# The first q transposed by DMA, the filter in six transfers, and a searched order at the start of a one-core attention and gating kernel

## Chip, cores and metric

One core of one Trainium2 chip. The metric is device microseconds (us) of one execution; lower is better. A run is told "slow" where it is more than 1.5% above the fastest run of the same kernel in the same comparison. The executions of this kernel scatter by 2 to 3% within one session, without a gap between fast and slow, so each comparison carries its own runs of the kernel before, on the same chip, and a 95% interval.

## The reference, cut

```python
def phi(x):                                   # q, k: [8 batches, 8 heads, 576, 64]; w_phi: [64, 128]
    proj = np.einsum('bhsd,df->bhsf', x, w_phi)
    proj = proj - np.max(np.abs(proj), axis=-1, keepdims=True)
    return np.concatenate([np.exp(proj), np.exp(-proj)], axis=-1)
q_p, k_p = (phi(q), phi(k))
kv = np.einsum('bhsf,bhsd->bhfd', k_p, v)     # one key-value product per head
z = np.sum(k_p, axis=2)
x = (q_p @ kv) / (q_p . z + 1e-6)             # shortened; then heads side by side: [8, 576, 512]
x1, x2, x3 = np.split(x @ w_proj, 3, axis=-1)
conv = irfft(rfft(x2, axis=1) * rfft(filter_fft, axis=0))   # filter_fft: [576, 512]
out = (x1 * conv * x3) @ w_out
```

## The kernel before

Every operation is a short method, and one long string of words, PLAN, gives the order in which they are issued; an engine, an index or a PSUM bank ("@4") stands in the word. Each engine takes its own instructions in that order. The parts that matter here:

```python
PLAN = """
zeros w_load,phi w_phi loadh,k,0,0 gen_rows gen_cols,1 loadh,k,0,1 gen_ident warm,10,4@0 T,k,0,0,1@0
gen_cols,0 Te,DVE,k,0,0,1@0 T,k,0,0,0@2 Te,ACT,k,0,0,0@2 filt_load,SP,1 warm,2,4@1 warm,3,1@1
T,k,0,1,0@4 loadh,q,0,0 Pk,0,0@0 Pk,0,1@2 ex,k,m,0,1@2 Te,ACT,k,0,1,0@4 gen_selidx loadh,q,0,1
load,k,1 gen_pads ... T,q,0,0,1@4 warm,5,4@5 T,q,0,1,1@5
Te,DVE,q,0,1,1@5 gen_turns,POOL,0 exkt,p,0@6 T,q,0,0,0@6 Te,DVE,q,0,0,1@4 T,q,0,1,0@4 ex,k,p,0,1@2
Te,ACT,q,0,0,0@6 warm,4,4@2 Qn,0,0@6 Te,ACT,q,0,1,0@4 load,v,0 ...
... load,q,1 ... vs,POOL,p,0,0 maxk,0,2@4 filt_load,SP,0 gen_sin,1 load,v,1 ...
vs,POOL,m,0,0 warm,18,4@6 warm,2,1@6 KV,0,0@4 KVe,DVE,0,0@4 trm,0 Pq,0,0@0 trh,q,1,1 ...
"""   # some 1,900 words more

def load(self, n, b):            # q, k or v of one batch from DRAM: 512 rows of 1152 B in bf16, on GpSimd's queue
    self.nc.gpsimd.dma_start(out=..., in_=...)          # loadh: half of the heads

def trh(self, n, b, X):          # a half of q or k, loaded before, transposed within SBUF, on SP's queue
    self.nc.sync.dma_start_transpose(out=self.at(n + "T", b)[:, 9 * X:9 * X + 9, :],
        in_=self.at(n + "n", b)[:, 2 * X:2 * X + 2].rearrange("p v j d -> p (v j d)"))

def T(self, n, b, X, i):         # the same on TensorE, for batch 0: matmuls with the identity
    ...
        self.mm(self.pb(k // 4 % 2, o, o + 128), x[:, c:c + 128], self.at("ident"), True, True)

def Te(self, eng, n, b, X, i):   # and the copy out of PSUM, by ACT or DVE
    ...

def filt_load(self, eng, i):     # one half of the filter, 9 transfers of 32 rows of 2048 B
    q = dict(SP=self.nc.sync, ...)[eng]
    rows = self.dram["filt"][288 * i:288 * i + 288, :].rearrange("(t j) d -> j t d", j=9)
    for k, j in enumerate((0, 2, 4, 6, 1, 3, 5, 7)):
        p = 32 * (k % 4)
        q.dma_start(out=self.fl[i][p:p + 32, k // 4, :], in_=rows[j])
    q.dma_start(out=self.fl[i][0:32, 2, :], in_=rows[8])
```

Qn is q's projection as the maxima need it, maxq the maxima of it, mhi/mlo and trm (mT) turn the maxima into an operand, Pq is the projection that the exponentials (ex) read, vs scales v on GpSimd, KV is the key-value product, warm is filler: matmuls on a tile "idle" that only keep the clock up.

## Time and profile before

| | kernel before |
|---|---|
| median of 3 runs, first session | 327.4 us (324.55 to 330.71) |
| span of the profiled execution | 320.2 us |
| TensorE (PE) busy / of it filler | 293.6 / 18.3 us |
| not useful PE time before 60 us / 60 to 300 / after 300 us | 30.4 / 7.3 / 7.2 us |
| filter transfers: number, KB, issue to landing | 18, 64.0 KB, 5.2 us |

"Not useful" is idle time plus filler. The lines for these are in the prediction below, read there. One view that it does not show: the queue of SP, the engine that issues all transposes and the filter's transfers. In the timeline of SP's queue (start, us that the issue itself took, line, operation, what, how many) the kernel before has:

```profile
2.00 3.85 SPq L420 DMA_DIRECT2D fl<-in_moe_filter_fft_dram  x8
6.81 6.12 SPq L420 DMA_DIRECT2D fl<-in_moe_filter_fft_dram  x8
...
26.47 1.19 SPq L679 DMA_TRANSPOSE mT<-mh  x1
27.76 2.72 SPq L545 DMA_TRANSPOSE qT<-qn  x2
30.57 3.56 SPq L545 DMA_TRANSPOSE kT<-kn  x2
```

The filter is off SP's hands at 13.4 us, and these transposes take 1.2 to 1.8 us each to issue.

### The profile page before, as it was taken

Reading aid. Unit: us, or ns where it says so; the run is one execution under the profiler, and the core shown is the slowest. Engines: PE = TensorE matmul, PEld = TensorE weight load, DVE = VectorE, ACT = ScalarE, POOL = GpSimd, SP = SyncE. Lnnn points to the kernel's source line nnn. Section 1 sums busy time; section 2 is a strip of 40 time slices with the busy share of each in tenths; the row PEclk is TensorE's granted clock in tenths of the full one; section 3 lists DMA queues with packets and bytes.
Section 4 is the critical chain, followed back from the end, with each engine's and each line's share of the span. In section 5 each row is a group of like instructions: output and inputs, shape, how many; then the busy total and the mean of one; then the engine's idle time right before and its main releaser. Section 6 shows DMA issues by size and latency. Waiting matters only on the chain.

```text
span 320.2 us, 9561 instructions
## 1 busy us (share of the span) xinstructions
PE 293.6 (92%) x3971; PEld 162.5 (51%) x3971; DVE 252.6 (79%) x416; ACT 229.4 (72%) x361; POOL 216.8 (68%) x175
## 2 busy tenths in 40 slices
PE   6659779999999899999799999999999999999982
PEld 2434643475465464475355554655566444764430
DVE  3584797699989997999478997888889988667860
ACT  2496999699788887897487875876788756843531
POOL 8769764967585962799084976938988589824140
PEclk9986987999999999999799999999999999999999
DMA  6999999969996999696943499787434410442506
GB/s 115 236 166 167 173 176 167 202 113 174 153 178 100 188 155 219 107 142 99 201 91 89 108 160 164 118 133 150 111 47 90 117 39 0 93 102 50 133 4 159
DMA packets 78667, 41.52 MB, mean 130 GB/s; under 512 B 58976, under 2 KB 73440, under 8 KB 78624
## 3 DMA queue, kind: packets, MB, share of 16 engines
q1 hardware_dynamic: 63808, 24.66, 40.1%
q0 software_dynamic: 14816, 16.25, 33.6%
q8 instruction: 31, 0.51, 0.7%
q14 instruction: 12, 0.10, 0.1%
HBM read 33.75 MB, written 9.44 MB: 135 GB/s over the span
## 4 chain that ended last, share of the span: by engine, by line
PE 74%; DVE 11%; ACT 5%; DMA 5%; issue 2%; POOL 0%; SPq 0%; ACTq 0%; DVEq 0%; POOLq 0%
PE ps L840 16%; PE ps L456 14%; PE ps L797 8%; PE ps L930 7%; PE ps L705 4%; PE ps L726 4%; DVE mq L650 4%; PE ps L296 3%; PE ps L847 2%; PE ps L611 2%; DMA kn<-in_k_dram 2%; DVE mk L650 2%; DMA mT<-mh 2%; PE ps L590 2%; PE ps L617 2%
## 5 line engine op out<-in xcount | busy, mean ns | idle before, releaser
L840 PE MATMUL ps<-xT,wproj 128*128 128x512 bf16 x256 | 64.3, 384 | 0.0
L907 POOL TENSOR_TENSOR yT<-cv,x1s 128x576 bf16<-128x576 f32 x22 | 27.9, 1276 | 36.1 <-DVE cv L897 20.3
L650 DVE TENSOR_REDUCE mq<-ps 128x8 f32<-128x1024 f32 (+1 forms) x40 | 44.0, 1111 | 5.8 <-PE ps L590 2.9
L650 DVE TENSOR_REDUCE mk<-ps 128x8 f32<-128x1024 f32 (+1 forms) x40 | 44.0, 1112 | 5.5 <-PE ps L583 4.5
L690 POOL TENSOR_TENSOR vp<-vn,vp 128x1152 bf16<-128x1152 bf16 x16 | 34.3, 2148 | 13.8 <-DVE yT L907 8.3
L827 POOL TENSOR_TENSOR t<-C,B 128x1024 bf16<-128x1024 bf16 x15 | 31.9, 2126 | 12.9 <-ACT C L710 6.2
L634 ACT ACTIVATE Eqp<-ps 128x1024 bf16<-128x1024 f32 x32 | 32.8, 1030 | 7.9 <-PE ps L617 7.7
L930 PE MATMUL ps<-wout,yT 128*128 128x512 bf16 x144 | 36.7, 380 | 1.4 <-DVE yT L907 0.9
L634 ACT ACTIVATE Ekm<-ps 128x1024 bf16<-128x1024 f32 x32 | 33.0, 1033 | 5.5 <-PE ps L583 4.6
L634 ACT ACTIVATE Eqm<-ps 128x1024 bf16<-128x1024 f32 x32 | 32.7, 1030 | 5.0 <-PE ps L617 4.3
L690 POOL TENSOR_TENSOR vm<-vn,vm 128x1152 bf16<-128x1152 bf16 x16 | 34.3, 2146 | 2.3 <-ACT es L892 1.5
L897 DVE TENSOR_TENSOR cv<-es,ps 128x288 f32<-128x288 f32 x64 | 25.8, 449 | 12.4 <-ACT es L892 10.9
L840 PEld LDWEIGHTS <-wproj 128*128 128x128 bf16 x256 | 22.8, 98 | 24.8 <-issue 1.4
L634 ACT ACTIVATE Ekp<-ps 128x1024 bf16<-128x1024 f32 x32 | 32.6, 1030 | 1.8 <-PE ps L583 1.1
L834 POOL TENSOR_TENSOR Y<-Y,t 128x1024 bf16<-128x1024 bf16 x14 | 29.7, 2123 | 1.9 <-DVE Y L822 1.3
L797 PE MATMUL ps<-wproj,eo 128*128 128x512 bf16 x128 | 29.9, 379 | 0.4 <-DVE eo L781 0.4
L456 PE MATMUL ps<-inv,Y 128*128 128x288 bf16 (+1 forms) x192 | 27.4, 291 | 0.2 <-DVE xnt L757 0.2
L710 ACT COPY o<-ps 128x512 f32<-128x512 f32 x27 | 15.7, 586 | 16.4 <-PE ps L930 11.8
L822 DVE TENSOR_TENSOR Y<-ps,A 128x1024 bf16<-128x1024 f32 (+1 forms) x24 | 24.8, 1041 | 3.0 <-PE ps L456 1.6
L877 DVE TENSOR_TENSOR x1s<-ps,x1s 128x512 bf16<-128x512 f32 x32 | 21.9, 686 | 5.1 <-PE ps L840 4.7
L745 DVE TENSOR_TENSOR xn<-ps,r 128x512 bf16<-128x512 f32 x32 | 22.0, 691 | 1.1
L710 ACT CAST x2n<-ps 128x512 bf16<-128x512 f32 (+1 forms) x28 | 14.5, 524 | 10.9 <-PE ps L797 8.8
(156 smaller groups left out, 632.4 us busy)
## 6 DMA issues: line engine op xcount, KB each, us to landing
out_dram<-o SPq DMA_DIRECT2D x72, 128.0 KB, 2.4
vn<-in_v_dram POOLq DMA_DIRECT2D x8, 576.0 KB, 6.4
kn<-in_k_dram POOLq DMA_DIRECT2D x7, 576.0 KB, 8.6
qn<-in_q_dram POOLq DMA_DIRECT2D x7, 576.0 KB, 7.0
wproj<-in_moe_w_proj_dram POOLq DMA_DIRECT2D x3, 512.0 KB, 7.1
fl<-in_moe_filter_fft_dram SPq DMA_DIRECT2D x18, 64.0 KB, 5.2
kn<-in_k_dram POOLq DMA_DIRECT2D x2, 288.0 KB, 5.7
qn<-in_q_dram POOLq DMA_DIRECT2D x2, 288.0 KB, 8.2
```

The source lines that it names most:

```text
L456: self.mm(self.pb(e, 0, n), l, r, start=(x == same[0]), stop=(x == same[-1]))
L634: self.nc.scalar.activation(e, self.db(), AF.Exp, bias=0.0, scale=1.0 if g == "p" else -1.0)
L650: self.nc.vector.tensor_reduce(out=out, in_=src, axis=AX.X, op=ALU.max, apply_absolute_value=True)
L690: self.port(eng, self.elem(eng).tensor_tensor(out=t[:, :, :, 0:64], in0=self.at("vn", b)[:, 2 * X:2 * X + 2], in1=t[:, :, :, 64:65].to_bro ...
L710: self.nc.scalar.copy(dst, src)
L797: self.mm(self.pb(0), eo[:, kt, 128 * c:128 * c + 128], w[:, kt, 512:1024], start=(kt == 0), stop=(kt == 3))
L827: self.port(eng, self.elem(eng).tensor_tensor(out=self.at("t2", b)[:, t, :], in0=self.at("C", b)[:, o, :], in1=self.at("B")[:, t, :], op=A ...
L834: self.port(eng, self.elem(eng).tensor_tensor(out=Y, in0=Y, in1=self.at("t2", b)[:, t, :], op=ALU.add))
L840: self.mm(self.pb(0), w[:, kt, f0 + 128 * m:f0 + 128 * m + 128], x[:, kt, :], start=(kt == 0), stop=(kt == 3))
L897: self.nc.vector.tensor_tensor(out=self.at("cv", 4 * b + m)[:, :, odd, :], in0=e, in1=o, op=ALU.subtract if odd else ALU.add)
L907: self.port(eng, self.elem(eng).tensor_tensor(out=self.at("yT", b)[:, m, 0:SEQ], in0=self.at("cv", 4 * b + m).rearrange("p j h t -> p (j h ...
L930: self.mm(self.pb(0), y[:, kt, 128 * j:128 * j + 128], w[:, kt, :], start=first and kt == ks[0], stop=last and kt == ks[-1])
```

## The change

Its intent is to shorten the start: take q's transposes and their copies off TensorE and ScalarE, spend less of SP on issuing, make the sine tables early, and load batch 1 before the first scaling of v. The core of the diff:

```diff
 def filt_load(self, eng, i):
-        for k, j in enumerate((0, 2, 4, 6, 1, 3, 5, 7)):
-            p = 32 * (k % 4)
-            q.dma_start(out=self.fl[i][p:p + 32, k // 4, :], in_=rows[j])
+        for odd in range(2):
+            q.dma_start(out=self.fl[i][:, odd, :], in_=rows[odd:8:2])
         q.dma_start(out=self.fl[i][0:32, 2, :], in_=rows[8])
 def T(self, n, b, X, i):            # k of batch 0 only, now
-            self.mm(self.pb(k // 4 % 2, o, o + 128), x[:, c:c + 128], self.at("ident"), True, True)
+            self.nc.tensor.transpose(self.turned(8)[:, o:o + 128], x[:, c:c + 128],
+                                     self.at("ident"))        # bf16, eight in one PSUM bank
 (B: four blocks become two; m3 subtracts for one of them)
 PLAN, first part
-...T,q,0,0,1@4 ... T,q,0,1,1@5 Te,DVE,q,0,1,1@5 ... T,q,0,0,0@6 ... (q of batch 0 on TensorE)
+zeros loadh,k,0,0 w_load,phi gen_rows gen_cols,0 gen_turns,ACT,0 loadh,q,0,0 loadh,k,0,1 gen_ident
+...
+Pkt,0@2 maxkt,0@2 load,v,0 load,q,1 gen_selidx ...
+em,p,0,0 vs,POOL,p,0,0 load,k,2 filt_load,SP,1 ...
+w_load,proj,1 trh,q,0,0 Qn,0,0@2 maxq,0,0@2 filt_load,SP,0 ...
+ex,k,m,0,2@6 trh,q,0,1 Qnt,0@2 ... mhi,0 trh,k,1,1 trh,k,1,0 ...
 (all of PLAN is in another order; filler falls from 53 wide and 17 narrow to 22 and 10)
```

On SP's queue the order is now: half of the filter, first half of q of batch 0, the other half of the filter, second half of q, both halves of k of batch 1, then q of batch 1 and the maxima.

## The prediction

> **What bounds the kernel now.** I read the page's totals first, then busy time by stage, the chain that ended last, and the timeline and the DMA view of the start. The totals say that TensorE is the engine to watch:
>
> ```profile
> PE 293.6 (92%) x3971; PEld 162.5 (51%) x3971; DVE 252.6 (79%) x416; ACT 229.4 (72%) x361; POOL 216.8 (68%) x175
> ...
> PEclk9986987999999999999799999999999999999999
> ```
>
> But 92% is an average over stages. The busy times by stage (length, PE, PEld, DVE, ACT, POOL, granted clock, DMA share, GB/s), first of everything and then of the tile "idle" alone, the operand of the filler matmuls that only keep the clock up:
>
> ```profile
> 0.00:6.00 6.00, 4.53 (x16) 1.67 (x17) 2.13 (x20) 1.28 (x1) 4.74 (x15) 1.00 0.53 93
> 6.00:30.60 24.60, 17.01 (x152) 8.96 (x149) 15.61 (x23) 17.91 (x26) 19.51 (x26) 0.86 1.04 187
> 30.60:47.00 16.40, 12.07 (x340) 9.60 (x338) 13.11 (x25) 14.46 (x18) 11.91 (x11) 0.97 1.20 177
> 47.00:60.00 13.00, 13.00 (x87) 5.18 (x87) 10.01 (x19) 9.62 (x21) 7.62 (x7) 0.78 1.25 180
> 60.00:90.00 30.00, 28.53 (x502) 17.25 (x501) 27.33 (x41) 26.38 (x40) 21.55 (x15) 1.00 1.04 155
> 90.00:300.00 210.00, 205.47 (x2815) 113.92 (x2809) 175.59 (x277) 154.35 (x247) 147.72 (x102) 0.99 0.64 117
> 300.00:320.20 20.20, 12.98 (x83) 5.90 (x81) 8.81 (x17) 5.41 (x11) 3.79 (x3) 0.97 0.40 94
> ```
> ```profile
> 6.00:30.60 24.60, 11.59 (x46) 4.78 (x46) 0.00 (x0) 0.86 1.04 187
> ...
> sum 320.20, PE 18.31 PEld 7.21 DVE 0.11; mean PE 2.62 PEld 1.03 DVE 0.02
> ```
>
> Useful TensorE work is 293.6 - 18.3 = 275.3 us, so 44.9 us of the span are not useful. In the first 60 us PE is busy 46.6 us, of which 17.0 us is filler: 30.4 us lost. From 60 to 300 us it is 6.0 idle plus 1.3 filler, 7.3 us. After 300 us it is 7.2 us. From 60 us on the kernel is simply TensorE bound and a shuffled order has little to win there. Two thirds of the loss is the start, and this change aims at the start.
>
> What holds the start? The chain in order of time (start, us, what):
>
> ```profile
> 2.88 6.93 DMA kn<-in_k_dram
> 9.85 0.62 PE ps L562 x8
> ...
> 16.29 1.83 ACT qT L710 x2
> ...
> 20.78 3.49 DVE mq L650 x3
> 24.31 6.39 PE ps L296 x20
> 30.70 1.26 PE ps L705 x72
> ```
>
> First the second half of k (landed at 9.85), then q's transposes and their copies, then VectorE's maxima; the filler (L296) up to 30.7 us only stands in PE's queue before the first key-value product. From 6 to 30.6 us DVE is idle 9.0, ACT 6.7 and POOL 5.1 of 24.6 us: batch 1 is not there yet. Its q is issued at 19.2 us and its transposes only at 27.8 us.
>
> **What the Trainium skill says.** (1) PSUM — Partial Sum Buffer, Specifications, engine access: a matmul writes fp32 "except transposes, which write the input dtype uncast"; that is what permits eight bf16 transposes in one bank. No transpose of the kernel before does this, so its trace does not show it. (2) TensorE: Matmul & The Clock Gate, Part 1: the clock falls to half after about 3.4 us without enough activity and recovers after about as long. The trace agrees: the granted clock was 0.86 over 6-30.6 us, and 0.78 over 47-60 us behind the thin work of 30-47 us. There 13.0 x 0.22 = 2.9 us of full-speed work was lost. (3) DMA: Bandwidth & Descriptors, "Why a DMA increments its semaphore by 16 and not by 1": a transfer uses the largest number of engines up to 16 that divides the slowest dimension of both sides. The old filter transfers have 32 rows on each side, so 16 engines. The new ones read 4 x 32 rows into 128 partitions, so by this rule 4 engines. No transfer of the kernel before has such a shape; its trace cannot say. (4) Advanced Engine Details and Errata, X-Bar Transpose (TRN2): transposes by DMA are as fast as ordinary ones. The trace agrees: 288 GB/s while a half of q or k is transposed (28-34 us), 230 GB/s for loads (14-19.5 us).
>
> **The change, part by part.**
> - q of batch 0 by DMA: removes 18 PE transposes (1.5 us busy), two 1024-wide ACT copies (1.9 us) and two small DVE ones (0.5 us), and adds two DMA transposes: 0.295 MB each at 288 GB/s is 1.0 us of the DMA engines, 1.3 us of the SP queue, and 3.1 us from issue to landing. It takes 1.8 us of ACT out of the chain but puts about 3 us after q's landing. The first q half is now loaded second, before k's second half, so this wait lies beside k's work. On the path: about -1 to -2 us.
> - bf16 transposes of k: same 18 matmuls, half the banks. The copies read the same 1024 elements; I expect the 1.01 us of ACT and 1.22 us of a DVE cast unchanged. Worth about 0; it frees a bank.
> - Filter in 6 transfers instead of 18: SP's queue spends 0.3-0.8 us on each, so about 6 us less of SP issue, and SP has q0's transposes to issue then. Bytes are the same, 1.18 MB.
> - B halved, subtraction instead of addition: two evictions of 0.59-0.69 us and half of a memset, once, about 1.3 us of ACT/DVE. The 2.13 us POOL multiplies and adds keep their size.
> - Filler: 53 wide and 17 narrow become 22 and 10. At 0.216 us per wide one that is about 7 us of PE, nearly all inside waits. Worth about 0, with a risk of a colder clock.
> - Order: the sine tables and both sine activations move before the first exponential, to where ACT waits for k; before, they take ACT from 22.0 to 27.8 us (two table loads of 1.28, activations of 0.68, 0.61, 0.24, 0.92) in the busiest part. That is worth 3-4 us there. Loads of v0, q1 and k2 are issued before POOL's first scaling, so batch 1 is projected ahead of the first key-value product.
>
> The sum of the start, by counting both orders with the durations above (reduce 1.18, exponential 1.0, scaling of v 2.14, product L705 1.2, 128-wide projection group 0.3, 512-wide group of four 0.86 us). Ahead of batch 2's first key-value product the kernel before has PE 48.1, DVE 69.0, ACT 72.1, POOL 67.6 us, and it is reached at 88.95 us. The changed one has PE 43.0, DVE 70.8, ACT 66.3, POOL 71.2 there; where its PE sum is 48.1, DVE is about 77, ACT 71, POOL 75. So 8 us more of DVE and 7 us more of POOL stand before the same TensorE work. In 0-90 us the kernel before has 68.2 us of DVE busy, so 22 us idle; the new order must cut these to about 10. With the first data at 5.7 us and about 6 us of table arithmetic done while waiting, DVE has some 71 us left from about 10 us on: 81 us with no gaps, 88 us at the 91% which it reached from 60 to 90 us. Between 1 and 8 us earlier; I take 4. Off that: the last matmuls have a little less to stand beside the last halves (two output groups instead of a projection pair and one), 1 us. Total -3 to -4 us of 327.
>
> **Rivals.**
> - A: the start is bound by DMA, and the new order shifts no bytes. From 6 to 60 us the DMA engines show a share of 1.04 to 1.25, i.e. never free. mT of batch 0 now stands on SP's queue behind the first transpose of q1, which waits for q1's load. Ten half loads at 1.28 us, 4.7 us of filter, 4 us of transposes after a start at 3.4 us give q1 at 25 us, as before (19.2 + 5.9). With the filter on 4 engines these would carry 2 x 64 packets more, about 67 ns each (estimate from packet times), 8.6 us instead of 2.4 us: q1 at 30 us, mT at 34 us, and the first query projection at 34 instead of 31.8 us. Then the time is 326-330 us. Against it: DMA has gaps after 25 us.
> - B: the start is bound by ACT and DVE arithmetic, and the order fills it. Then 316-320 us. For it: ACT 9.1 of 10 us busy from 20 to 30 us. Against it: DVE needs over 91%.
> - C: POOL becomes the bound. Eight scalings of v, 17 us, now precede the first filter matmul instead of five, and folds of batches 0 and 1 moved from DVE (0.65 us) to POOL (2.13 us). That would make about 325 us.
> - D: less filler, colder clock: a second stretch at 0.6-0.8 for 10 us costs up to 3 us; 326 us.
>
> **Range and chances.** The reference is 327.4 us, with runs 324.55 to 330.71, a scatter of 2% by itself. The middle is 327.4 - 3.9 = 323.5 us. B at its best gives 316; A and D together give 330. More than 2% needs 6.5 us off, nearly all of B: 0.23. Slower by 2% needs A, D and a worse end: 0.07. Within 2%: 0.70.
>
> **What would show it.** Right: PE's waste before 60 us falls from 30.4 to about 26 us; the first key-value product starts at 26-28 instead of 30.6 us; batch 2's first starts about 8-9 us sooner (5 us of PE work moved behind it); from 90 to 300 us PE is busy 97-99% again. A is shown by filter transfers that land after 8 us or more (5.2 now) and by q1 landing near 30 us; C by DVE or PE waiting on scaled v or on POOL's folds; D by PEclk at 5-7 in several slices before 70 us. The prediction is wrong if the start gains more than 6 us because the exponentials never wait, or if TensorE gets bubbles in the middle, where the reshuffled engines of 70 other copies could cost what the start won.

## The result, and the profile after

Ratios in this document are the mean time of one kernel's fast runs over that of the other's of the same rounds, so they are not quite the ratio of the medians that are quoted.

| | before | after |
|---|---|---|
| median in the comparison | 329.05 us (324.55 to 332.45, 4 runs) | 340.99 us (340.71 to 344.13, 4 runs) |
| ratio | | 1.0482, 95% interval 1.0352 to 1.0613: slower |
| span of the profile, granted clock | 320.2 us, 0.971 | 339.4 us, 0.906 |
| PE busy / filler / useful | 293.6 / 18.3 / 275.3 us | 286.4 / 9.5 / 276.9 us |
| not useful before 60 us | 30.4 us | 45.6 us |
| 60 to 90 us / 90 to 300 us / end | 2.7 / 4.5 / 7.2 us | 8.5 / 1.5 / 7.0 us |

All four runs after are fast ones, and the slowest run before (332.45 us) is still below the fastest after. Busy times by stage of the changed kernel (length, PE, PEld, DVE, ACT, POOL, granted clock, DMA share, GB/s), to be held against the seven lines of the prediction, and the filler's sum below them:

```profile
0.00:6.00 6.00, 4.63 (x13) 1.50 (x14) 3.44 (x26) 2.78 (x4) 4.76 (x15) 1.00 0.47 80
6.00:30.60 24.60, 7.13 (x68) 4.02 (x66) 10.50 (x15) 12.81 (x20) 14.79 (x18) 0.71 1.27 162
30.60:47.00 16.40, 2.82 (x36) 1.90 (x36) 4.74 (x5) 3.13 (x5) 0.00 (x0) 0.50 1.06 117
47.00:60.00 13.00, 8.07 (x159) 6.61 (x160) 9.55 (x15) 8.09 (x13) 9.48 (x8) 0.50 0.86 137
60.00:90.00 30.00, 22.49 (x447) 14.81 (x444) 19.90 (x30) 18.55 (x26) 17.95 (x15) 0.71 1.20 176
90.00:300.00 210.00, 208.87 (x3001) 118.91 (x3001) 181.90 (x289) 166.65 (x264) 164.90 (x111) 1.00 0.75 120
```
```profile
sum 339.40, PE 9.50 PEld 3.17 DVE 0.11; mean PE 1.19 PEld 0.40 DVE 0.01
```

The stage from 30.6 to 47 us is the striking one: every engine stands still for most of it (VectorE is busy 4.74 of 16.4 us), GpSimd for all of it. Something that no engine does is missing. The middle, 90 to 300 us, is even fuller than before (208.87 of 210 us). So the loss is 15.2 us in the first 60 us and 5.7 us in the next 30, with 3 us won back later. The 19.2 us of the span are these: 15.2 + 5.7 - 3.0 - 0.2, and 1.6 us more of useful PE time.

What was missing is told by SP's queue after (columns as before):

```profile
1.99 1.27 SPq L417 DMA_DIRECT2D fl<-in_moe_filter_fft_dram  x2
...
12.00 1.87 SPq L541 DMA_TRANSPOSE qT<-qn  x1
13.91 3.51 SPq L417 DMA_DIRECT2D fl<-in_moe_filter_fft_dram  x2
17.47 3.49 SPq L418 DMA_DIRECT2D fl<-in_moe_filter_fft_dram  x1
21.08 10.38 SPq L541 DMA_TRANSPOSE qT<-qn  x1
31.56 13.16 SPq L541 DMA_TRANSPOSE kT<-kn  x2
44.82 2.18 SPq L541 DMA_TRANSPOSE qT<-qn  x1
49.31 1.13 SPq L676 DMA_TRANSPOSE mT<-mh  x1
```

To issue the second half of q of batch 0 took 10.4 us, where a half of q of batch 1 took 1.4 us before; k of batch 1 took 13.2 us; and the maxima's transpose comes at 49.3 instead of 26.5 us. The landing is later still. For the transposes of q that were issued before 60 us (three of the four have a landing in the trace):

```profile
DMA to landing us min/median/max: 4.3/22.6/22.7
```

The two halves of batch 0 are the 22.7 and the 22.6: issued at 12.0 and 21.1 us, they landed at 34.7 and 43.7 us, where the prediction had 3.1 us from issue to landing. The first key-value product, which the prediction expected at 26 to 28 us, started at 48.8 us (30.6 before). The chain that ended last, in order of time (start, us, what), runs through exactly these:

```profile
2.88 9.11 DMA qn<-in_q_dram
12.00 1.87 SPq L541
...
21.08 10.38 SPq L541
31.56 7.91 SPq L541
39.52 8.62 DMA kT<-kn
...
66.73 13.58 DMA qT<-qn
```

Before, this chain went through PE, ACT and DVE after the first load. What the DMA engines did meanwhile is seen in the DMA view from 25 to 37 us (mean busy share of the 16 engines in tenths, a digit for each 0.3 us, and GB/s), first before, then after:

```profile
DMA  9869999999992599919998199939900799999999
GB/s 54 50 92 169 192 196 207 211 192 223 200 179 50 133 288 288 253 26 224 288 288 177 44 275 289 338 76 144 31 9 9 153 207 292 268 140 143 174 195 184
```
```profile
DMA  2222222222222222232232232232232999999999
GB/s 72 67 75 72 67 75 72 67 75 72 83 99 96 102 109 102 96 79 70 65 79 70 65 79 70 65 79 64 63 63 47 71 76 73 91 74 75 82 76 82
```

After, the mean share is 0.2 to 0.3 for nearly 10 us: that is what a quarter of the engines would make, with all the work, at 65 to 80 GB/s for most of it. The trace's packet records agree: from 25 to 34.6 us, four or five packets are in flight for 8.7 of the 9.6 us. The landings of the filter:

```profile
DMA to landing us min/median/max: 11.8/15.1/18.4
```

These are two transfers only, the one of 64 KB at the end of each half, which landed at 15.1 and 35.9 us; for the four of 256 KB this profile has no landing. Before, each of the 18 landed 3.5 to 6.7 us after its issue. That SP's long issue comes of these crowded engines is inferred from the two happening at the same time; experiment 13 limits it.

### The profile page after: what moved, and what is told of

Same layout as the page of the kernel before. It is cut to its first block, busy times and chain, and to the rows that moved or that the text cites. A ratio compares the mean times of both kernels' runs of the same rounds, so it can differ in the third digit from the quotient of the medians.

```text
span 339.4 us, 9427 instructions
## 1 busy us (share of the span) xinstructions
PE 286.4 (84%) x3915; PEld 162.4 (48%) x3915; DVE 254.2 (75%) x420; ACT 227.0 (67%) x357; POOL 217.7 (64%) x169
## 4 chain that ended last, share of the span: by engine, by line
PE 71%; DMA 13%; SPq 8%; DVE 2%; ACT 2%; issue 1%; POOL 0%; POOLq 0%; ACTq 0%
PE ps L836 16%; PE ps L453 12%; PE ps L794 8%; PE ps L926 8%; DMA qT<-qn 7%; PE ps L702 6%; SPq L541 6%; PE ps L723 4%; DMA qn<-in_q_dram 3%; DMA kT<-kn 3%; PE ps L587 2%; PE ps L608 2%; PE ps L843 2%; PE ps L580 2%; PE ps L614 2%; PE ps L437 1%
## 5 line engine op out<-in xcount | busy, mean ns | idle before, releaser
L836 PE MATMUL ps<-xT,wproj 128*128 128x512 bf16 x256 | 63.2, 379 | 0.1
L687 POOL TENSOR_TENSOR vm<-vn,vm 128x1152 bf16<-128x1152 bf16 x16 | 34.4, 2152 | 24.7 <-DVE mh L672 19.7
L903 POOL TENSOR_TENSOR yT<-cv,x1s 128x576 bf16<-128x576 f32 x24 | 30.5, 1277 | 29.4 <-DVE x1s L873 11.2
L631 ACT ACTIVATE Ekp<-ps 128x1024 bf16<-128x1024 f32 x32 | 32.8, 1031 | 19.7 <-DVE mk L647 12.2
L687 POOL TENSOR_TENSOR vp<-vn,vp 128x1152 bf16<-128x1152 bf16 x16 | 34.4, 2149 | 11.5 <-ACT vp L681 10.4
L824 POOL TENSOR_TENSOR t<-C,B 128x1024 bf16<-128x1024 bf16 x13 | 27.5, 2124 | 5.9 <-DVE C L709 3.1
L794 PE MATMUL ps<-wproj,eo 128*128 128x512 bf16 x128 | 31.0, 380 | 0.0
L587 PE MATMUL ps<-wphi,qT 64*128 64x128 bf16 x256 | 14.3, 245 | 18.5 <-DMA qT<-qn 16.4
L778 POOL TENSOR_TENSOR eo<-xT 128x1024 bf16<-128x1024 bf16 x10 | 21.2, 2127 | 10.7 <-DMA xT<-xn 9.7
L829 POOL TENSOR_TENSOR Y<-Y,t 128x1024 bf16<-128x1024 bf16 x12 | 25.4, 2122 | 3.9 <-DVE Y L819 2.5
L707 ACT COPY o<-ps 128x512 f32<-128x512 f32 x28 | 16.4, 587 | 12.2 <-PE ps L926 9.2
## 6 DMA issues: line engine op xcount, KB each, us to landing
kn<-in_k_dram POOLq DMA_DIRECT2D x7, 576.0 KB, 11.1
```

The source lines that it names most:

```text
L631: self.nc.scalar.activation(e, self.db(), AF.Exp, bias=0.0, scale=1.0 if g == "p" else -1.0)
L687: self.port(eng, self.elem(eng).tensor_tensor(out=t[:, :, :, 0:64], in0=self.at("vn", b)[:, 2 * X:2 * X + 2], in1=t[:, :, :, 64:65].to_bro ...
L794: self.mm(self.pb(0), eo[:, kt, 128 * c:128 * c + 128], w[:, kt, 512:1024], start=(kt == 0), stop=(kt == 3))
L824: self.port(eng, self.elem(eng).tensor_tensor(out=self.at("t2", b)[:, t, :], in0=self.at("C", b)[:, o, :], in1=self.at("B"), op=ALU.mult))
L829: self.port(eng, self.elem(eng).tensor_tensor(out=Y, in0=Y, in1=self.at("t2", b)[:, i:i + 3:2, :], op=ALU.add if i else ALU.subtract))
L836: self.mm(self.pb(0), w[:, kt, f0 + 128 * m:f0 + 128 * m + 128], x[:, kt, :], start=(kt == 0), stop=(kt == 3))
```

## Experiments

Two parts are under suspicion: the filter's new shape, and q by DMA; the order, the filler and the small parts are the others. "18 transfers" and "6 transfers" are the filter's old and new form. Fifteen kernels ran, in five groups, each with its own runs of the kernel before. In 1, 3, 4, 9, 11 and 12 it is "unclear": the interval lies above 1 but not wholly above 1.02. The first key-value product's start is given where it helps; it is read from the one profiled execution, which in 3, 4, 7, 8, 13, 14 and 15 was a slow one.

### 1. The changed kernel with the old filter transfers

```diff
-        for odd in range(2):
-            q.dma_start(out=self.fl[i][:, odd, :], in_=rows[odd:8:2])
+        for k, j in enumerate((0, 2, 4, 6, 1, 3, 5, 7)):
+            p = 32 * (k % 4)
+            q.dma_start(out=self.fl[i][p:p + 32, k // 4, :], in_=rows[j])
```

> The changed kernel with the filter again in 18 transfers of 32 rows; nothing else is touched. Theory 1 (the six transfers have a slowest source dimension of 4, use 4 of 16 DMA engines, and the transposes queued behind them wait): the stretch from 21.5 to 37 us with a DMA share of 2 tenths and 70 GB/s goes, k's first-batch-1 transposes land 12 us or more sooner, the wait of PE for qT falls from 16 to under 6 us, and the time falls from 341 to 324-329 us. Theory 2 (the transposes share the DMA engines packet by packet with the loads that were moved ahead of them): the share is high anyway, the time stays at 335-341 us. Theory 3 (less filler, so a colder clock is the cause): the clock stays at 0.5 from 30 to 60 us and the time stays over 335 us.

Measured: 331.61 us median (fast 329.01 to 333.03), ratio 1.0138 (1.0016 to 1.0259) to the kernel before. So of 4.8% some 3.4 points, about 11 us, are the filter's shape; theories 2 and 3, which left the time over 335 us, fall as its cause. The stretch of 0.2 went and the first key-value product came at 40.5 instead of 48.8 us. But the time stayed above theory 1's 324 to 329 us, and two other signs stayed as in the changed kernel: TensorE waited for q's transposes 13.8 and 8.5 us in the first 90 us (15.8 and 6.7 there), and the clock was 0.50 from 30.6 to 47 us again. A remainder stays. SP's queue shows where:

```profile
8.54 1.81 SPq L542 DMA_TRANSPOSE qT<-qn  x1
10.40 13.58 SPq L418 DMA_DIRECT2D fl<-in_moe_filter_fft_dram  x8
...
24.64 1.98 SPq L542 DMA_TRANSPOSE qT<-qn  x1
```

Eight filter transfers took 13.6 us behind the first transpose, where they took 6.1 us before, and q's second half waited until 24.6 us.

### 2. The kernel before with the new filter transfers alone

```diff
-        for k, j in enumerate((0, 2, 4, 6, 1, 3, 5, 7)):
-            ... (one transfer of 32 rows each)
+        for odd in range(2):
+            q.dma_start(out=self.fl[i][:, odd, :], in_=rows[odd:8:2])
```

> The kernel before with only the filter in six transfers. There no transpose is queued behind the filter until 26 us, and all of the filter is issued at the start. Theory 1: loads finish late on four engines; the second half of k lands about 2-3 us later than 9.85 us, q's halves and k of batch 1 4-6 us later; the time is 3-8 us over the kernel before, 331-336 us. Theory 2: within 1 us of the kernel before.

Measured: 331.84 us median of four runs (327.0 to 337.73); only two count as fast. Beside 327.1 us of the kernel before, the medians put it 4.7 us higher, the two fast runs 3.1 us. In the order of the kernel before nothing stands behind the filter on SP for long. If the same shape costs less there, what queues up behind it matters; these runs hint at that and do not show it.

### 3. The six transfers on ScalarE's queue instead of SP's

```diff
-zeros loadh,k,0,0 ...  load,k,2 filt_load,SP,1 ...  maxq,0,0@2 filt_load,SP,0 ...
+zeros filt_load,ACT,1 filt_load,ACT,0 loadh,k,0,0 ...  load,k,2 ...  maxq,0,0@2 ...
```

> The changed kernel with its six filter transfers issued from ScalarE's queue at the very start, so that the transposes, on SP's queue, no longer stand behind them in the same ring, while the same four engines still carry all of the filter. If the loss comes of standing behind the filter in the queue: the issue of the second half of q's transpose falls from 10.4 us to under 4 us and the time falls by 8 us or more, to 325-333 us. If it comes of the four engines being overloaded, whatever the queue: loads and transposes still land late, and the time stays over 335 us.

Measured: 335.14 us median, two fast runs at 332.12 and 332.32, ratio 1.0183 (1.0055 to 1.031). By the fast runs, issuing earlier and off SP's queue is worth some 9 us, as the queue theory said; but that theory's own sign failed: in the profile (a slow run) q's two halves still take 13.9 us to issue from 12.0 us on, and ScalarE does nothing for 10.2 us while it issues. Which of the two, the queue or the earlier start, gave the gain is not separated, and the interval overlaps that of experiment 1.

### 4. The changed kernel with q of batch 0 on TensorE again

```diff
-... trh,q,0,0 Qn,0,0@2 ... trh,q,0,1 Qnt,0@2 ...
+... T,q,0,0,1@4 T,q,0,0,0@5 Te,DVE,q,0,0,1@4 Te,DVE,q,0,0,0@5 Qn,0,0@2 ...
+... T,q,0,1,0@4 T,q,0,1,1@5 Te,DVE,q,0,1,0@4 Te,DVE,q,0,1,1@5 Qnt,0@2 ...
```

> The changed kernel with q of batch 0 transposed by TensorE again (two copies per half, by DVE), the filter still in six transfers. SP then issues the whole filter at the start and its first transposes are those of k of batch 1. Theory 1: the filter still slows the loads (k's second half lands at 12-16 us) but nothing waits 20 us behind it: 328-336 us. If the DMA transpose of q is itself the cause, whatever the filter: 323-329 us, as for the kernel before or better. If neither: 338-342 us.

Measured: 334.91 us median, fast 333.22 to 336.2, ratio 1.0248 (1.0136 to 1.036). Q by DMA is therefore worth some 2.3 points of the loss while the filter is slow.

### 5. Both taken back

The edits of 1 and 4 together; the order, the bf16 transposes, half B and little filler stay.

> The changed kernel with two parts taken back: 18 filter transfers, and q of batch 0 transposed on TensorE again; bf16 transposes of k and of q, half B, little filler and the new order stay. So against the kernel before it is the order, the bf16 transposes and B alone. Theory Q (what is left of the loss beyond the filter's shape is the SP queue: a transpose of q0 stands there behind 18 filter transfers, and each transpose takes 4 to 10 us to issue and to land): 325 to 328 us where the kernel before has 327. Theory O (the new order itself costs, because VectorE, ScalarE and GpSimd are used up in another sequence and GpSimd's first scaling stands 13 us waiting with the later loads behind it): 331 to 334, no better than the 331.6 us with 18 filter transfers alone.

Measured: 326.85 us median (324.91 to 327.59, all fast), ratio 1.0004 (0.9938 to 1.0069). The whole loss is gone, and there is no gain: the new order with its small parts is worth nothing measurable. The first key-value product started at 30.0 us (30.6 before; 35.9 in experiment 4). With experiments 1, 2, 4 and 9 this fills a table of ratios to the kernel before:

| | 18 transfers | 6 transfers |
|---|---|---|
| new order, q on TensorE | 1.0004 | 1.0248 |
| new order, q by DMA | 1.0138 | 1.0482 |
| old order, q on TensorE | 1 | (1.01, two fast runs, no interval) |
| old order, q by DMA | 1.0156 | not run |

Each of the two alone costs; together they cost a little more (4.8%) than the product of the two (1.0248 x 1.0138 = 1.039), though the intervals leave that open.

### 6 and 7. The 18 transfers ahead of q's transposes; and loads of batch 1 later

```diff
 (6)  vs,POOL,p,0,0 load,k,2 filt_load,SP,1 filt_load,SP,0 ...  trh,q,0,0 Qn,0,0@2 maxq,0,0@2 ...
 (7, on top of 6)
-maxkt,0@2 load,v,0 load,q,1 gen_selidx ... gen_five ex,k,m,0,1@4
+maxkt,0@2 gen_selidx ... gen_five load,v,0 load,q,1 ex,k,m,0,1@4
```

> The changed kernel with 18 filter transfers and all of them put ahead of q0's transposes on SP's queue (in the run with 18 alone nine of them stood between q0's two halves and took 13.6 us to issue, so the second half was issued at 24.6 us). Theory Q: the second half of q0 is issued before 17 us, k1's transposes before 21 us, and the time is 326 to 329 us. Theory S (transposes and the loads that were moved ahead share the 16 DMA engines packet by packet, and whichever is issued first the bytes take until 30 us): the transposes are issued sooner but land as late, and the time stays 330 to 332. Theory O: 330 to 333.

> As the run with the 18 filter transfers ahead, and besides v of batch 0 and q of batch 1 issued some 6 us later, behind GpSimd's selector copies (about 15.5 us instead of 9.7 us). Theory S: q0's second half lands 3 us or more sooner and the time falls by 2 us or more against the run without this. Theory Q: within 1.5 us of it. Theory O: the same or 1 to 3 us slower, since batch 1 arrives later.

Measured for 6: q's two halves were issued from 13.3 us on, in 8.7 us, and k's by 27.2 us; 327.1 and 330.38 us in its two fast runs, ratio 1.0071 (0.9965 to 1.0176), but two more runs at 339.14 and 341.14. For 7: 328.04 us in one fast run, three slow ones up to 352.69. Freeing SP's queue may help, perhaps by half of the remainder, but the interval overlaps that of experiment 1; in the profile the second half's issue began at 14.8 us, as theory Q wanted, but took 7.2 us, so k's came after its 21 us. Whether the loads matter is not told by these, because the runs scatter more than the effect.

### 8. Only the small parts, in the order of the kernel before

PLAN of the kernel before in the code of the changed one, with 18 transfers.

> The order of the kernel before, whole, in the code of the changed one with 18 filter transfers: so only the bf16 transposes into one PSUM bank, with their cheaper copies for k and for q of batch 0, and the halved B. Worked out from the profiles, this saves two DVE copies of 0.53 us on each of k and q at most and two evictions, some 1 to 2 us of DVE and ACT, not all of it on the path: 325 to 327 us where the kernel before has 326 to 327. If it is under 324, the small parts are worth something that the new order gives back; if it is over 328, the narrow bank use costs. Theory Q and theory O have no stake here except this: theory O says that all of the loss of the order is paid for by a gain here, so it expects 322 to 324; theory Q says that order and small parts are each about nothing, 325 to 327.

Measured: fast runs 322.02 to 326.24 us (median of all six 327.44), ratio 0.9942 (0.986 to 1.0024): within 2% of the kernel before, a gain of about half a per cent not excluded and not shown. The DVE copy of eight bf16 transposes took 0.69 us in the profile of the changed kernel.

### 9. The kernel before with q of batch 0 by DMA alone

```diff
-T,q,0,0,1@4 warm,5,4@5 T,q,0,1,1@5 Te,DVE,q,0,1,1@5 ... (and the other T and Te of q)
+trh,q,0,0 warm,5,4@5 trh,q,0,1 ...      (and filt_load,SP,0 right behind filt_load,SP,1)
```

> The kernel before with one part alone: q of batch 0 transposed by two DMAs instead of on TensorE; all 18 filter transfers stand ahead of them on SP's queue. The prediction gave this part -1 to -2 us: 325 to 326 where the kernel before has 327. Theory Q and theory S: the transposes take 6 us or more from issue to landing beside the loads of k1 and the filter, so TensorE gets its first query product later than the copies gave it, and the time is 328 to 332 us. Theory O: about 327.

Measured: 332.22 us median, fast 330.02 to 333.04, ratio 1.0156 (1.0053 to 1.026): about +5 us where the prediction had -1 to -2. The chain (start, us, what) shows the term itself:

```profile
13.54 1.35 SPq L545
...
14.99 12.51 DMA qT<-qn
```

This is the second half: issued at 15.0, it landed at 27.5 us. The first, issued at 13.5, landed after 9.0 us, at 22.5 us. In the kernel before, q's copies out of PSUM were done at 18.1 us (16.29 and 1.83 us in the prediction's chain). The term of 3.1 us from issue to landing, read from transposes at quieter times, was 9.0 and 12.5 us here, and the first key-value product started at 39.8 us. The 20 filler matmuls that stand ahead of it in PLAN took 6.2 us of that chain; whether q by DMA would cost less without them was not tried.

### 10 and 11. Two tries on top of experiment 5

```diff
 (10)
-trh,q,1,0 Qn,1,0@6 maxq,1,0@6 ex,k,p,1,0@4 trm,0 Pq,0,0@2 trh,q,1,1
+trh,q,1,0 Qn,1,0@6 maxq,1,0@6 trh,q,1,1 ex,k,p,1,0@4 trm,0 Pq,0,0@2
 (11)
+warm,12,4@2 (ahead of Qn,0,0)   warm,16,4@6 (ahead of Qn,1,0)
```

> As the run with both parts taken back, but with the second transpose of q of batch 1 put ahead of the transpose of batch 0's maxima on SP's queue (there it was issued at 31.8 us, behind the maxima, and TensorE stood 5.5 us until 38.05 us for it). Theory Q (SP's queue decides the start): issued near 26 us instead of 31.8, landing before 35 us, 1 to 3 us faster than that run: 323 to 326 us. Theory S: the bytes arrive no sooner, because the loads fill the engines until then; 326 to 327. If the maxima's transpose is what comes late instead (it stands behind a slow issue), 327 to 329.

> As the run with both parts taken back, with 28 filler matmuls of 512 columns put in again, 12 ahead of the first query projection and 16 ahead of the first projection of q of batch 1, both places where TensorE waits. Rival D of the prediction (less filler, colder clock): the granted clock, 0.57 over 30.6 to 47 us in that run, comes to 0.8 or more and the time falls by 1 to 3 us, to 324 to 326. If the cold stretch is only waiting for transfers, filler raises the clock and the time stays within 1 us, at 326 to 328; where the filler stands in front of work that was ready, it costs 1 to 3 us.

Measured for 10: 326.07 us median, ratio 0.9947 (0.9872 to 1.0022); the transpose was issued by 30.6 us and PE's waits for q fell from 13.2 to 9.6 us. For 11: 331.25 us, ratio 1.0165 (1.0095 to 1.0236). The stage from 30.6 to 47 us of experiment 5, then of 11 (columns as in the stage tables above):

```profile
30.60:47.00 16.40, 9.69 (x236) 7.93 (x230) 10.54 (x17) 10.28 (x14) 12.40 (x10) 0.57 1.32 157
```
```profile
30.60:47.00 16.40, 12.15 (x197) 8.38 (x198) 12.46 (x19) 11.02 (x17) 8.27 (x7) 0.77 0.77 128
```

The clock came up from 0.57 to 0.77, and the kernel was about 5 us slower than experiment 5: the filler stands ahead of work in PLAN, and the maxima's transpose was issued at 36.5 instead of 30.6 us. The cold clock in these 16 us goes with the waiting; curing it this way did not pay.

### 12. Experiment 9 with less traffic beside q's transposes

```diff
-filt_load,SP,1 filt_load,SP,0 ... load,k,1 ... trh,q,0,0 warm,5,4@5 trh,q,0,1 gen_turns,POOL,0 ...
+... trh,q,0,0 warm,5,4@5 trh,q,0,1 filt_load,SP,1 filt_load,SP,0 gen_turns,POOL,0 load,k,1 ...
```

> The kernel before with q of batch 0 transposed by DMA (the run that did this alone: first half issued at 13.54 us, landed at 27.50 us, 330 to 333 us), now with the traffic beside the transposes taken away: all 18 filter transfers stand behind the two transposes on SP's queue, and the load of k of batch 1 behind GpSimd's table, some 7 us later. Theory S (the transposes are slow because loads and filter share the DMA engines with them): both transposes issue in under 4 us together, the first half lands within 6 us of its issue, before 21 us, and the time falls by 2 us or more, to 326 to 329. Theory Q (SP's queue, not the traffic): nothing stands ahead of them on that queue in either run, so they take as long as before and the time stays 330 to 333, or grows because the filter is late.

Measured: both transposes issued in 2.77 us from 10.61 us, they landed after 3.0 and 6.7 us (9.0 and 12.5 in experiment 9), and q's projection ran from 16.2 us instead of 22.6. So other transfers are what makes these transposes slow: that part is shown. Which ones is not, for two things were moved at once. (Two slips in the expectation: the 13.54 and the 27.50 us are of different halves, and in experiment 9 something does stand ahead on SP's queue, all 18 filter transfers.) But the time was 332.1 us, ratio 1.0127 (1.0051 to 1.0203), no better. The chain now goes through other waits:

```profile
13.20 12.03 DMA vn<-in_v_dram
...
37.29 9.55 DMA kT<-kn
```

The bytes that had been moved out of the way were then late themselves. My expectation for the time (326 to 329 us) was wrong.

### 13. The changed kernel, its filter rows read in another order

Same six transfers, same bytes, same rows of 2048 B; only the slowest dimension of the DRAM side is 32 instead of 4. The filter lands on other partitions, so its rows are mixed (the comparison with the reference passed all the same, so here that comparison vouches for nothing).

```diff
+        mixed = rows[0:8].rearrange("j t d -> t j d")
         for odd in range(2):
-            q.dma_start(out=self.fl[i][:, odd, :], in_=rows[odd:8:2])
+            q.dma_start(out=self.fl[i][:, odd, :], in_=mixed[:, odd:8:2, :])
```

> The changed kernel, whole, with its six filter transfers, but each large one reads its 128 rows in the order 32 by 4 instead of 4 by 32: same number of transfers, same bytes, same 2048 B rows, another slowest dimension (32 instead of 4). The filter's rows land on other partitions, so the result is wrong on purpose. Theory T1 (the slowest dimension of 4 puts all rows on 4 of the 16 engines): the stretch at 70 to 77 GB/s with a DMA share of 0.2 is gone, the filter's transfers land within 8 us, and the time is that of the run with 18 transfers, 327 to 333 us. Rival L (large transfers are slow by their size, or because few of them stand behind each other, whichever rows they read): the stretch stays and the time is 338 to 343 us as in the changed kernel.

Measured: fast runs 327.02, 328.23 and 331.34 us, ratio 1.0037 (0.9934 to 1.0139), against 1.0482 for the changed kernel. The DMA view from 25 to 37 us, of a slow run:

```profile
DMA  9999369999999999999999913999999999999999
GB/s 401 349 312 172 54 148 289 281 288 289 304 201 230 188 227 200 200 231 235 197 188 257 52 13 22 98 65 62 68 79 102 129 147 141 167 177 188 196 195 166
```

The stretch of 0.2 is gone, and in the packet records sixteen or more packets are in flight for most of it. Number and size of the transfers are innocent; the outermost 4 was the fault. Two signs of the slow run hold a warning: the second half of the filter landed after 11.9 to 13.0 us, not within 8 (the first half after 4.4 to 6.2), and SP still took 7.0 us to issue q's second half. So a long issue is not the mark of the four engines alone.

### 14 and 15. Transposes that nobody reads, and the same in earnest

On experiment 8: two DMA transposes of q into an unread tile, with q still done on TensorE (14); then those two in earnest, without the TensorE ones (15).

```diff
 (14) +trdummy,q,0,0 T,q,0,0,1@4 warm,5,4@5 trdummy,q,0,1 T,q,0,1,1@5 ...
 (15) +trh,q,0,0 warm,5,4@5 trh,q,0,1 ...
```

> The order of the kernel before with the small parts (that run was 0.994 of the kernel before) with q of batch 0 still transposed on TensorE, and besides it two DMA transposes of the same q into a tile that nothing reads, at the place where the DMA would do it in earnest. Only the traffic is added, no wait for it. Theory S, traffic (the transposes' own packets and what they hold up in the loads of k1, v0 and the filter is the cost): 328 to 332 us, nearly all of what the real thing costs. Theory W, latency (the cost is that TensorE waits for q, landed 9 us later than the copies had it): 324 to 327 us, nothing or little.

> The same code with q of batch 0 transposed by those two DMAs in earnest, and the TensorE transposes and their copies gone. Both theories: 328 to 332 us, as the kernel before with this one part (1.016 of the kernel before). Beside the run with the unread transposes it gives the share of traffic and of waiting on the same chip. If it is within 1 us of the kernel before, the cost seen in that other run was not the transposes.

Measured: 14 gave 326.2, 326.6 and 329.89 us fast, ratio 1.0158 (0.9982 to 1.0334): unclear, as the kernel before had only two fast runs in this group (321.21 and 323.72). 15 gave one fast run, 331.05 us, and three from 337 to 339 us. By the lowest run of each, 321.2, 326.2 and 331.1 us, traffic and wait would have equal shares, but that rests on single runs, and the medians hold slow ones. The profiles (all slow) say something of the start: the first key-value product came at 29.5 us in 14 and at 41.2 us in 15 (32.2 in experiment 8), so the unread transposes did not delay it and the wait did. The shares of the whole time are not settled.

## Why the prediction was wrong

It said 323.5 us and 7% for slower; the kernel is 4.8% slower. By its own steps:

- **What bounds the kernel** held. The losses, 15.2 and 5.7 us, lie before 90 us; the end stayed at 7.0 us (7.2), and the middle rose to 99.5% as hoped.
- **"Filter in 6 transfers instead of 18 ... Bytes are the same"** is the step that failed most. The prediction had cited the rule that gives these transfers 4 engines, and then booked the part as a saving of SP's time and left the rule to rival A. Experiments 1, 4 and 5 put the part at 2.4 to 3.4% (8 to 11 us), and experiment 13 shows that the slowest dimension does it. Nor did SP save the 6 us: its issue of the filter took 8.9 us, after 11.1. A sum of the right size, with a rate known only afterwards: four transfers of 256 KB are 1.05 MB; at the 75 GB/s of the slow stretch that is 14 us, at the 230 GB/s of ordinary loads 4.6 us, so 9.4 us apart (an estimate, from these measured rates).
- **Rival A** named the mechanism, slow filter transfers with q1 and mT behind them, and gave it 326 to 330 us. Its load of q1 at 30 us was right: it landed at 28.8 us. What follows was mis-sized: mT was issued at 49.3 us, not 34. What it left out is SP's queue: q's second half took 10.4 us and k1's two took 13.2 us to issue there, so q1's transpose, whose data had lain ready since 28.8 us, was issued at 44.8 us.
- **"q of batch 0 by DMA ... On the path: about -1 to -2 us"** was wrong in sign: +5 us alone (experiment 9), 1.3 to 2.3% in the new order. This is the second step that failed. It took the 3.1 us from issue to landing of quiet transposes; it was 9.0 and 12.5 us in experiment 9, and 22.7 and 22.6 us in the changed kernel. (The 288 GB/s beside it was read from the fullest slices; the mean of that stretch, 28 to 34 us, is 180 GB/s.)
- **Order, -3 to -4 us**: the sum itself is loose ("I take 4", less 1, is 3, not 3.9). Experiment 5 gives 1.0004. The order with the small parts is worth between -2.0 and +2.3 us of 327 by its interval. So the gain that the count of engine work promised did not come. What the count leaves out is waits for transfers: in experiment 5, too, PE waits for q's transposes (of batch 1, 13.2 us in two waits). That these waits ate the gain is likely and not shown.
- **bf16 transposes and half B, about 0 and 1.3 us**: within the interval of experiment 8. "Unchanged" copies were right for ScalarE (1.006 us) and wrong for VectorE (0.69 instead of 1.22 us).
- **Rivals B, C and D**: B (the start is bound by ScalarE and VectorE, 316 to 320 us) fell: no run shows a gain. C fell as well: GpSimd itself waited, 19.7 us in one wait for VectorE's maxima. D was seen (clock 0.50 from 30.6 to 60 us), beside the waiting; more filler made experiment 5 slower. Its share in the changed kernel itself was not measured.
- **What would show it** was well chosen: "filter transfers that land after 8 us or more" (11.8 and 18.4) and q1 landing near 30 us (28.8) are just what the profile has.

Open: how q by DMA splits into traffic and waiting, and whether its cost and the filter's add or multiply. No run beat both kernels beyond its interval; experiments 8 and 10 (0.994 and 0.995) are the nearest.

## What to carry to other kernels

Before merging transfers, write down the outermost dimension of both sides: a merge that put a 4 outermost moved the same bytes over a quarter of the engines here, and loads and transposes of the same time came late with it. Read the time of a DMA transpose from a moment with the traffic that it will really meet, not from the median of the page. And if a prediction cites a rule that speaks against a part, work that rule into the sum of the part, not into a rival.

## What the Trainium skill lacked or had wrong

- DMA: Bandwidth & Descriptors, "Why a DMA increments its semaphore by 16 and not by 1" (the largest number of engines up to 16 that divides the slowest dimension of both sides) agrees with these runs: share 0.2 to 0.3 and 65 to 80 GB/s with a slowest dimension of 4, ratio 1.0482, and 1.0037 with 32. What it lacks is the cost to others: other loads of the same time landed late too (k of batch 2 and a third of the projection's weights after 17.5 us each), and one issue of SP took 10.4 us.
- The same page, "Rules for kernel authors", advises to coalesce many small transfers into one large one. Here 18 transfers of 64 KB landed after 5.2 us (median); with the merged ones the last of each half landed after 11.8 and 18.4 us, and the part cost 2.4 to 3.4%. The row should point to the row "Use all 16 engines" of the same table, which has the condition.
- The same rules say "A transpose next to ordinary DMAs needs nothing". For correctness no run contradicts this; for time, two transposes beside other transfers took 9.0 and 12.5 us to land (experiment 9), and 3.0 and 6.7 us where these had been moved (experiment 12).
- Advanced Engine Details and Errata, "X-Bar Transpose (TRN2)": transposes "are as fast as regular DMAs". In a quiet stretch the runs agree (288 GB/s before); in the loaded start the same kind of transpose decided the chain (12.51 us in experiment 9), a case of which the section says nothing.
- None of the pages that I drew on gives the time that SP takes to issue a transpose beside other traffic: 1.3 to 1.9 us in quiet stretches, 10.38 us in the changed kernel, 7.0 us in experiment 13.
